# Attention in two blocks: two other strings for the order of TensorE's visits and of the projections in the first block

## The chip, the cores and the metric

The kernel runs on one core of one Trainium2 chip. The metric is the device time of one execution in microseconds (us); lower is better. TensorE multiplies matrices into PSUM (8 banks), ScalarE and VectorE read PSUM, GpSimd works on SBUF, and SyncE issues the DMAs in one queue.

## What is computed

Two independent attention layers with 2048 tokens, width 512 and 32 heads of 16 dimensions; the outputs stand side by side. Layer A sees a sliding window of 256 tokens, layer B sees all tokens.

```python
qkv = (x @ wqkv).reshape(B, S, 3, H, Dh)          # S 2048, H 32, Dh 16
scores = einsum("bhqd,bhkd->bhqk", q, k) * Dh**-0.5
mask = (i - j >= 0) & (i - j < 256)               # layer A alone
p = softmax(scores)
out = einsum("bhqk,bhkd->bhqd", p, v) ... @ wo
```

## The kernel before, in words

**Two stages.** In the first block TensorE does layer A's attention and the projections (q, k, v) of both layers. Then a loop does layer B's attention with an order of its own (the strings `MANY`, `FEW`, `OUTS`, `ENDS`). The change touches the first block alone.

**A string sets TensorE's order.** `ORDER_A` has 761 letters, and each letter is one visit of TensorE. The loop over it takes the letters one by one and emits that visit's matmuls; nothing is reordered afterwards.

- `p`: one projection, 12 matmuls of 128x512 on the whole array (line 309). It takes the next name of `ORDER_P`.
- `g`: a quarter of two projections at once, 12 matmuls on the two halves of the array (line 444). Four `g` make two projections; it takes two names.
- `m`: scores for the row maxima, 2 matmuls into two banks (line 607; the first ones of layer B, also `e`, line 561). VectorE then copies under a mask and reduces (lines 616, 617).
- `t`: two small transposes of a unit's maxima (line 681). ScalarE copies the result to `ntr` (line 683), and two DMAs of SyncE (line 688) put it as three extra rows into the q tile `oq`.
- `s`: scores of a pair of heads into two banks (line 717), which need those rows of `oq`. ScalarE takes the exponential (line 724), GpSimd masks it.
- `w`: weights times values, on column groups of the array (line 764).

A unit is one group of four heads and one chunk of 512 queries; layer A has 32 units. Each has one `t`, six `s`, three `w` and eight `m`. Names such as `Av21` in `ORDER_P` read: layer A, v, chunk 2, tile 1; `Ak02` is k of heads' group 0, chunk 2.

**What follows from the order.** The same walk over the string emits the work of the other engines: when a projection ends, ScalarE copies it out of its bank, VectorE or GpSimd splits it, SyncE stores it; loads are emitted when the kernel's own clock (class `Model`) says that they are due. So the two strings also decide where in the queues of ScalarE, VectorE, GpSimd and SyncE each of these stands, and which of the 7 free banks a visit writes. Each queue is worked off in order. `m` and `s` take two banks each, so three such visits fill six of the seven.

Of the kernel before, what the change touches and what calls it, by code (L numbers as in the profile page):

```python
# [57 lines left out]
FILL = 16  # L58
WARM = 22
ORDER_P = (  # L60
# [4 lines left out]
    "Bq20 Bq12 Bk30 Bk31 Bk10 Bq33 Bq30 Bq31 Bk32 Bq32 Bk33 Bk21 ").split()  # L65
WAKE = 200
GAP_V = 1500
PIECE = 4
# [4 lines left out]


ORDER_A = (
    "pppppppppppmmmmpmmgmgmptmgmgmmpmsgmsgmmpmsgmsgmwtsmgmsgmmpmsgsmgmtwwmmmpsmgmsgmswwmsgmsgmmpmssptwsmg"
    "msgmswsmgsmgmmwwmgmsgmstwmsgmsgmmwtsgmsgmswmsgmsgmswmmmpssmtwwmspmsmwssmgsmgmswtmsgsmgmwsmswssmwmmmp"
    "mtmswmsswmsmpsmmpsmwtmmmpsmswmmspmsmwsmsmwwtmsmsmsmpmsmtwsmsmwsmmswssmwmmspmmswsmwtsmgmsgmswsmgsmtgm"
    "mwsmwsmmswsmsmpsmmwmswtmsmwsmmmpmsssmmwsmsmwtmmmpsmswmsmsmwtsmsmwsmmpmmswsmtwmmmpmsgmsgmswtsmgmswpsm"
    "gsmwwmsgmmgmpmsgmsgsmwwtsmgmsgmswsmgsmgmmwtsgsmgsmwwmsgmsgmgsmgmswsmgmmgmwsmwtmsgmsgmswtmsgsmgmswwsm"  # L80
    "gmsgmswsmgsmgsmtwwmmmpmsmpmsmwsmmswtmsgmsgmswsmgsmgsmwmsmtwsmmswssmwmmmpmssmtwswmmmpmsgsmgsmwwmsgsmg"
    "etwmmmpmsgmsgmswsegsmgegesgmswsmgesgemtwmmpmsmwmswmsgsmgestwmsgesgmmpemmpmsmwwtemmpsmgmsgsmwmgegsewm"
    "mmpesstwmgmsgeswsmgsmgsmwesgsmgsmwmgsmgmswesmpsmmwtwmmmpmmmwp")
LAND = 400
LAND_V = 0
LGAP = 2500
# [1296 lines left out]
```

## Time and profile before

| what | value |
|---|---|
| device time, median of 3 runs | 1776.86 us (1775.77 to 1780.85) |
| device time of the profiled execution | 1775.89 us |
| its span | 1774.2 us |
| TensorE busy | 1756.8 us (99%) |
| VectorE busy | 1527.2 us (86%) |
| ScalarE busy | 1402.2 us (79%) |
| GpSimd busy | 648.5 us (37%) |
| TensorE's granted clock | full in each of the 40 slices |

A matmul counts as busy from its start to its modelled end, and neighbours overlap, so a share of 99% does not say that TensorE never waits. The length of a visit is better read as the time from its first matmul's start to the next visit's first start. A row of the timeline has its start, its length, the engine, the line, the operation and what was merged (xcount); in brackets stands idle time ahead of it and what ended that.

### The profile page before, as it was taken

How to read it: one execution, taken by the hardware profiler on the slowest of the kernel's cores; microseconds unless marked ns; L12 is line 12 of the kernel's file. 1: busy time of each engine (PE TensorE's matmuls, PEld its weight loads, DVE VectorE, ACT ScalarE, POOL GpSimd, SP SyncE). 2: the span in 40 equal slices, each digit the busy share in tenths (PEclk: the TensorE clock that was granted, in tenths of full speed). 3: DMA queues.
4: the chain of work that ended last, by engine and by line, in shares of the span. 5: the costliest groups of instructions: out<-in, count | busy, mean ns of one | idle time of the engine just before them, and what ended most of it. 6: DMA issues, size and time to landing. Idle time of an engine off the chain costs nothing.

```text
span 1774.2 us, 38875 instructions
## 1 busy us (share of the span) xinstructions
PE 1756.8 (99%) x14774; PEld 912.2 (51%) x14774; DVE 1527.2 (86%) x2386; ACT 1402.2 (79%) x2749; POOL 648.5 (37%) x1334
## 2 busy tenths in 40 slices
PE   8999999999999999999999999999999999999999
PEld 6776657767754444444444444444444444444456
DVE  4766786676779999999999999999999999999921
ACT  4466676665569888888889999999999999899894
POOL 0377888655755441222201123231112322121420
PEclk9999999999999999999999999999999999999999
DMA  8865667645663224111310311120031131010012
GB/s 267 200 210 199 206 206 223 177 146 163 201 181 108 66 86 89 41 41 41 83 37 17 77 29 30 47 62 17 17 78 35 30 65 38 17 38 26 20 44 102
DMA packets 129354, 166.78 MB, mean 94 GB/s; under 512 B 23204, under 2 KB 59044, under 8 KB 129156
## 3 DMA queue, kind: packets, MB, share of 16 engines
q1 hardware_dynamic: 129168, 164.31, 31.8%
q8 instruction: 116, 1.90, 0.5%
q14 instruction: 70, 0.57, 0.1%
HBM read 94.49 MB, written 68.19 MB: 92 GB/s over the span
## 4 chain that ended last, share of the span: by engine, by line
PE 89%; DVE 4%; DMA 2%; ACT 1%; SPq 1%; issue 1%; POOL 1%; POOLq 0%; ACTq 0%; DVEq 0%
PE ps_all L749 28%; PE ps_all L717 19%; PE ps_all L561 18%; PE ps_all L444 11%; PE ps_all L309 6%; PE ps_all L764 4%; DVE mt L564 3%; PE ps_all L607 3%; ACT p L724 1%; DMA in<-xT_A 1%; DVE nm L617 1%; PE ps_all L681 0%; SPq L473 0%; DVE ps_all L616 0%; DMA parts<-st 0%
## 5 line engine op out<-in xcount | busy, mean ns | idle before, releaser
L724 ACT ACTIVATE p<-ps_all 128x512 f32<-128x512 f32 x2432 | 1262.9, 598 | 204.8 <-PE ps_all L717 137.6
L564 DVE TENSOR_REDUCE mt<-ps_all 128x1 f32<-128x512 f32 (+1 forms) x1658 | 1212.7, 808 | 33.1 <-PE ps_all L561 28.0
L717 PE MATMUL ps_all<-oq,opk 51*128 51x512 f32 (+2 forms) x2752 | 756.9, 401 | 4.0 <-ACT p L724 2.0
L561 PE MATMUL ps_all<-opk,oq 48*128 48x512 f32 x2016 | 661.2, 435 | 0.2
L749 PE MATMUL ps_all<-p,vt 128*17 128x512 f32 (+1 forms) x5488 | 571.0, 490 | 0.0
L717 PEld LDWEIGHTS ps_all<-oq,opk 51*128 51x128 f32 x2752 | 385.8, 185 | 219.2 <-ACT p L724 142.7
L561 PEld LDWEIGHTS ps_all<-opk,oq 48*128 48x128 f32 x2016 | 304.6, 184 | 273.4 <-DVE mt L564 164.7
L735 POOL TENSOR_SCALAR_AFFINE_SELECT p<-p 128x256 f32<-128x256 f32 x480 | 179.0, 408 | 110.0 <-ACT p L724 107.4
L749 PEld LDWEIGHTS ps_all<-p,vt 128*17 128x17 f32 x5488 | 93.6, 95 | 214.2 <-issue 201.4
L616 DVE COPY_PREDICATED ps_all<-mone,ps_all 128x256 f32<-128x256 uint16 x224 | 95.3, 425 | 82.6 <-PE ps_all L607 75.9
L617 DVE TENSOR_REDUCE nm<-ps_all 128x2 f32<-128x512 f32 x224 | 155.2, 693 | 7.7
L633 POOL TENSOR_TENSOR mu<-mt 128x16 f32<-128x16 f32 x31 | 6.9, 222 | 409.9 <-DVE mt L564 409.9
L635 POOL TENSOR_TENSOR mu<-mt,mm 128x16 f32<-128x16 f32 x62 | 13.6, 220 | 388.7 <-DVE mt L564 388.7
L444 PE MATMUL ps_all<-x,w 64*128 64x512 f32 x720 | 119.2, 392 | 0.0
L444 PE MATMUL ps_all<-w_o,x_o 64*128 64x512 f32 x576 | 110.2, 394 | 0.0
L309 PE MATMUL ps_all<-x,w 128*128 128x512 f32 x408 | 102.7, 400 | 2.4 <-ACT x L257 1.7
L764 PE MATMUL ps_all<-p,vt 128*17 128x384 f32 (+2 forms) x1408 | 94.1, 386 | 0.1
L607 PE MATMUL ps_all<-opk,oq 48*128 48x384 f32 (+2 forms) x512 | 92.1, 361 | 2.0 <-DMA oq<-parts 0.5
L803 POOL TENSOR_TENSOR rd<-ld,minus 128x32 f32<-128x32 f32 x15 | 81.9, 5459 | 19.6 <-DMA ld<-od 19.6
L444 PEld LDWEIGHTS ps_all<-x,w 64*128 64x128 f32 x720 | 84.4, 185 | 8.9
L309 PEld LDWEIGHTS ps_all<-x,w 128*128 128x128 f32 x408 | 74.2, 188 | 24.8 <-ACT p L724 2.9
L392 ACT ACTIVATE raw<-ps_all 128x512 f32<-128x512 f32 x56 | 32.2, 596 | 68.5 <-PE ps_all L309 53.6
(79 smaller groups left out, 1042.7 us busy)
## 6 DMA issues: line engine op xcount, KB each, us to landing
parts<-st SPq DMA_DIRECT2D x64, 512.0 KB
oq<-parts SPq DMA_DIRECT2D x128, 128.0 KB
opk<-parts SPq DMA_DIRECT2D x128, 128.0 KB
od<-ou SPq DMA_DIRECT2D x64, 256.0 KB
vd<-vst SPq DMA_DIRECT2D x32, 272.0 KB
oq<-parts SPq DMA_DIRECT2D x128, 64.0 KB
opk<-parts SPq DMA_DIRECT2D x128, 64.0 KB
t<-od SPq DMA_DIRECT2D x32, 256.0 KB
```

Source lines behind the costliest of these rows:

```text
L309: nc.tensor.matmul(ps, l(u), r(v), start=start and k == 0, stop=stop and k == n - 1)
L444: op = nc.tensor.matmul(ps[a ^ turn], l(u)[rows], r(v)[rows], start=turn == q == 0, stop=turn == 1 and q == 11)
L561: nc.tensor.matmul(ps[:, a - lo], q[rows, 128 * qt:128 * qt + 128], k[rows, kc * QC:kc * QC + QC], start=True, stop=True)
L564: op = nc.vector.tensor_reduce(out=m[:, kc, lo:lo + len(sides), r, qt], in_=ps, axis=AX.X, op=ALU.max)
L607: nc.tensor.matmul(two[:, a, 0:w], opq[b, g, c][rows, r, 128 * qt:128 * qt + 128], opk2(g)[rows, r, t0:t1], start=True, stop=True)
L616: nc.vector.copy_predicated(two[:, :, 256:384], later, two[:, :, 0:128])
L617: op = nc.vector.tensor_reduce(out=m[:, :, r, qt, 0], in_=two[:, :, 128:384], axis=AX.X, op=ALU.max)
L717: nc.tensor.matmul(ps[x][:, col:col + n1], opk2(g)[rows, pr, 128 * k:128 * k + 128], opq[b, g, c][rows, pr, q0:q0 + n1], start=True, stop= ...
L724: op = nc.scalar.activation(p[:, a0 + x, :w], ps[x][:, :w], AF.Exp, scale=SCALE)
L735: nc.gpsimd.affine_select(out=v, in_=v, pattern=[[0, 2], [sign, 128]], compare_op=ALU.is_ge, fill=zero_fill, base=base, channel_multiplier ...
L749: nc.tensor.matmul(o[32 * j:32 * j + VW, q0:q1], vt[(g // 2) % 2][:, kt, vc:vc + VW], pts[1, g, c, kt, j // 2][:, j % 2, q0:q1], start=kt ...
L764: nc.tensor.matmul(o[32 * j:32 * j + VW, q0:q0 + w], vt[(g // 2) % 2][:, kt, vc:vc + VW], pts[b, g, c, m, j // 2][:, j % 2, col:col + w], ...
```

## The change

`ORDER_P` and `ORDER_A` are two other strings. Both orders have the same letters (280 `m`, 192 `s`, 96 `g`, 96 `w`, 48 `p`, 33 `t`, 16 `e`) and the same 96 names of projections; nothing else in the file differs. The two first lines of each show the kind of edit:

```diff
 ORDER_P = (
-    "Aq00 Ak00 Ak01 Av11 Av02 Av03 Aq01 Av01 Ak02 Av21 Av13 Aq02 Av12 Av00 Aq03 Ak03 Av20 Av10 Av33 Ak20 Av32 "
+    "Aq00 Ak00 Aq01 Av13 Av01 Av03 Aq02 Ak01 Av11 Av20 Av12 Ak02 Av02 Av00 Aq03 Ak03 Av23 Av31 Av21 Aq12 Av30 "
...
 ORDER_A = (
-    "pppppppppppmmmmpmmgmgmptmgmgmmpmsgmsgmmpmsgmsgmwtsmgmsgmmpmsgsmgmtwwmmmpsmgmsgmswwmsgmsgmmpmssptwsmg"
+    "ppppppppmmpmmppmgmmgmptmgmmgmppsmgsmgmmpmsgmsgmtwmsgmsgmmpmsgmsgmtwwmmmpmsgmsgsmwwmsgmsgmmpssmptwmsg"
```

After the first block the rows of every engine are the same in both programs, up to the numbers of buffers.

**TensorE near the start, before.** The last of eleven projections in a row (L309), then the first `m` (L607), for the first unit's q tile.

```order
L309 MATMUL ps_all<-w_v_225,x_2_3_255 128x512 x3
L309 MATMUL ps_all<-w_v_207,x_1_0_168 128x512 x3
L309 MATMUL ps_all<-w_v_210,x_1_1_171 128x512 x3
L309 MATMUL ps_all<-w_v_222,x_1_2_189 128x512 x3
L309 MATMUL ps_all<-w_v_225,x_1_3_192 128x512 x3
L607 MATMUL ps_all<-opk_75,oq_0_0_268 128x128 x4
L607 MATMUL ps_all<-opk_75,oq_0_0_268 128x256 x4
L309 MATMUL ps_all<-x_2_0_239,w_0_0_139 128x512 x3
L309 MATMUL ps_all<-x_2_1_242,w_0_0_139 128x512 x3
L309 MATMUL ps_all<-x_2_2_252,w_0_0_139 128x512 x3
L309 MATMUL ps_all<-x_2_3_255,w_0_0_139 128x512 x3
L607 MATMUL ps_all<-opk_75,oq_0_0_268 128x384 x4
```

**The same place after.** Four `m` now stand in pairs between projections, the first pair behind the eighth projection.

```order
L607 MATMUL ps_all<-opk_75,oq_0_0_268 128x128 x4
L309 MATMUL ps_all<-w_v_207,x_1_0_168 128x512 x3
L309 MATMUL ps_all<-w_v_210,x_1_1_171 128x512 x3
L309 MATMUL ps_all<-w_v_222,x_1_2_189 128x512 x3
L309 MATMUL ps_all<-w_v_225,x_1_3_192 128x512 x3
L607 MATMUL ps_all<-opk_75,oq_0_0_268 128x256 x4
L309 MATMUL ps_all<-w_v_207,x_2_0_239 128x512 x3
L309 MATMUL ps_all<-w_v_210,x_2_1_242 128x512 x3
L309 MATMUL ps_all<-w_v_222,x_2_2_252 128x512 x3
L309 MATMUL ps_all<-w_v_225,x_2_3_255 128x512 x3
L309 MATMUL ps_all<-w_v_207,x_1_0_168 128x512 x3
```

The two first pairs moved apart, and earlier: one projection now stands between them, where before they followed each other.

**TensorE at the unit whose q tile is `oq_2_2` (heads' group 2, chunk 2), before.** The `t` of this unit (L681), then seven `s` and `m` in a row, then a projection.

```order
L681 MATMUL ps_all<-ident,nm_74 32x128
L607 MATMUL ps_all<-opk_75,oq_2_3_2210 128x384 x2
L717 MATMUL ps_all<-oq_2_1_1854,opk_75 128x256 x4
L607 MATMUL ps_all<-opk_75,oq_2_3_2210 128x384 x2
L717 MATMUL ps_all<-oq_2_1_1854,opk_75 128x256 x4
L607 MATMUL ps_all<-opk_75,oq_2_3_2210 128x384 x2
L717 MATMUL ps_all<-oq_2_1_1854,opk_75 128x384 x2
L717 MATMUL ps_all<-oq_2_1_1854,opk_75 128x128 x2
L607 MATMUL ps_all<-opk_75,oq_2_3_2210 128x384 x2
L309 MATMUL ps_all<-x_2_0_239,w_3_0_1298 128x512 x3
```

**The same `t` after.** Values (L764) now stand between the `s` and `m` that follow it.

```order
L681 MATMUL ps_all<-ident,nm_74 32x128
L717 MATMUL ps_all<-oq_2_1_1858,opk_75 128x128 x2
L717 MATMUL ps_all<-oq_2_1_1858,opk_75 128x384 x2
L607 MATMUL ps_all<-opk_75,oq_2_3_2205 128x384 x4
L717 MATMUL ps_all<-oq_2_1_1858,opk_75 128x128 x2
L717 MATMUL ps_all<-oq_2_1_1858,opk_75 128x384 x2
L764 MATMUL ps_all<-p_2_0_1_0_2371,vt_78 17x384 x2
L764 MATMUL ps_all<-p_2_0_1_1_2378,vt_78 17x384 x2
L607 MATMUL ps_all<-opk_75,oq_2_3_2205 128x384 x2
L717 MATMUL ps_all<-oq_2_1_1858,opk_75 128x256 x4
```

The run of seven is broken. The first `s` with this unit's rows follows 25 rows further on before, and 36 after.

**TensorE a little later, after.** The `t` of the next unit (`oq_2_3`) and one visit of values are followed by eight `s` and `m` in a row.

```order
L717 MATMUL ps_all<-oq_2_2_2036,opk_75 128x128 x2
L717 MATMUL ps_all<-oq_2_2_2036,opk_75 128x384 x2
L607 MATMUL ps_all<-opk_76,oq_3_0_2451 128x256 x2
L717 MATMUL ps_all<-oq_2_2_2036,opk_75 128x128 x2
L717 MATMUL ps_all<-oq_2_2_2036,opk_75 128x384 x2
L607 MATMUL ps_all<-opk_76,oq_3_0_2451 128x256 x2
L717 MATMUL ps_all<-oq_2_2_2036,opk_75 128x256 x4
L607 MATMUL ps_all<-opk_76,oq_3_0_2451 128x384 x2
L717 MATMUL ps_all<-oq_2_2_2036,opk_75 128x256 x4
L607 MATMUL ps_all<-opk_76,oq_3_0_2451 128x384 x2
L764 MATMUL ps_all<-p_2_1_2_0_2552,vt_78 17x384 x2
```

Before, that `t` and its `w` were followed by four `s` and `m` up to the next `w`; now it is eight.

## Rows read from the trace of the kernel before

**Rows 1.** Busy time of each engine before and after the first block's last matmul; clock, DMA

```profile
core 0: us, PE busy (x) PEld busy (x) DVE busy (x) ACT busy (x) POOL busy (x), PEclk, DMA share, GB/s
0.00:515.60 515.60, 504.61 (x4520) 359.46 (x4520) 357.35 (x763) 303.15 (x605) 330.08 (x644) 1.00 0.65 198
515.60:1774.00 1258.40, 1252.23 (x10255) 552.75 (x10254) 1169.85 (x1623) 1099.09 (x2144) 318.47 (x690) 1.00 0.19 51
```

**Rows 2.** TensorE's timeline: the block's first matmul and the loop's first one

```profile
6.70 0.50 PE L309 MATMUL ps_all<-x,w 128*128 128x512 f32 x1 [1.15 <-ACT x L257]
...
515.62 0.50 PE L717 MATMUL ps_all<-oq,opk 51*128 51x512 f32 x2
```

**Rows 3.** TensorE's timeline, a stretch without crowding; start, length, what

```profile
218.63 0.50 PE L717 MATMUL ps_all<-oq,opk 51*128 51x256 f32 x4
218.97 0.40 PE L607 MATMUL ps_all<-opk,oq 48*128 48x384 f32 x2
219.20 1.54 PE L444 MATMUL ps_all<-x,w 64*128 64x512 f32 x12
220.58 0.34 PE L607 MATMUL ps_all<-opk,oq 48*128 48x384 f32 x2
220.75 0.40 PE L717 MATMUL ps_all<-oq,opk 51*128 51x384 f32 x4
220.99 1.60 PE L444 MATMUL ps_all<-x,w 64*128 64x512 f32 x12
...
222.59 0.41 PE L717 MATMUL ps_all<-oq,opk 51*128 51x384 f32 x4
222.93 1.06 PE L764 MATMUL ps_all<-p,vt 128*17 128x128 f32 x16
223.92 0.44 PE L717 MATMUL ps_all<-oq,opk 51*128 51x384 f32 x2
```

**Rows 4.** TensorE's timeline near the start, 30 to 42 us

```profile
30.44 2.88 PE L309 MATMUL ps_all<-x,w 128*128 128x512 f32 x12
33.16 2.88 PE L309 MATMUL ps_all<-w_v,x 128*128 128x512 f32 x12
37.25 3.01 PE L309 MATMUL ps_all<-w_v,x 128*128 128x512 f32 x12 [1.21 <-DVE st L399]
40.19 0.60 PE L607 MATMUL ps_all<-opk,oq 48*128 48x128 f32 x5
...
41.78 3.02 PE L309 MATMUL ps_all<-x,w 128*128 128x512 f32 x12
```

**Rows 5.** Timelines of SyncE, ScalarE and VectorE in the same place

```profile
24.49 2.23 SPq L473 DMA_DIRECT2D opk<-parts  x4
...
33.38 2.41 ACT L257 ACTIVATE x<-in 128x512 fp32r<-128x512 f32 x4 [1.17 <-DMA in<-xT_A]
...
36.51 0.68 DVE L399 TENSOR_TENSOR st<-ps_all,st 128x512 fp32r<-128x512 f32 x1
```

**Rows 6.** Timelines of TensorE and SyncE, and TensorE's waits over the first block

```profile
194.14 0.23 PE L681 MATMUL ps_all<-ident,nm 128*32 128x128 bf16 x2
...
201.40 1.08 PE L764 MATMUL ps_all<-p,vt 128*17 128x128 f32 x16
203.62 0.74 PE L717 MATMUL ps_all<-oq,opk 51*128 51x128 f32 x4 [1.15 <-DMA oq<-ntr]
...
200.74 1.50 SPq L688 DMA_DIRECT2D oq<-ntr  x2
...
PE ps_all L717 <- DMA oq<-ntr: 1.1, 1, 1.1
```

**Rows 7.** TensorE's timeline in a crowded stretch

```profile
194.29 0.45 PE L607 MATMUL ps_all<-opk,oq 48*128 48x384 f32 x2
...
196.97 0.50 PE L717 MATMUL ps_all<-oq,opk 51*128 51x384 f32 x4 [0.48 <-ACT p L724]
...
197.62 3.02 PE L309 MATMUL ps_all<-x,w 128*128 128x512 f32 x12
```

More of the change, by code (lines that the diff above doesn't have):

```diff
@@ L60 @@
 ORDER_P = (
[4 rows of a table removed]
-    "Bq20 Bq12 Bk30 Bk31 Bk10 Bq33 Bq30 Bq31 Bk32 Bq32 Bk33 Bk21 ").split()
[4 rows of a table added]
+    "Bq22 Bq10 Bq23 Bk30 Bq30 Bq31 Bk31 Bk32 Bk10 Bq33 Bq32 Bk33").split()
 WAKE = 200
@@ L75 @@
 ORDER_A = (
-    "pppppppppppmmmmpmmgmgmptmgmgmmpmsgmsgmmpmsgmsgmwtsmgmsgmmpmsgsmgmtwwmmmpsmgmsgmswwmsgmsgmmpmssptwsmg"
[L77 to L83, printed above, removed]
+    "ppppppppmmpmmppmgmmgmptmgmmgmppsmgsmgmmpmsgmsgmtwmsgmsgmmpmsgmsgmtwwmmmpmsgmsgsmwwmsgmsgmmpssmptwmsg"
+    "msgmswsmgsmgmmwwmsgsmgmstwmsgmmgwsmgmsgmswtsmgmsgsmwsmmpmswtwsmmpsmsmwmsgmsgmswtmsgsmgmwsmswsmsmwmsm"
+    "pmmswtmswsmmpmsmpsmtwmmmpmsswmmspmmswtsmmswmsmswsmmpmmswtwsmsmsmsmwmsswmsmpmsmwmswtmsgmgmswsmgmsgmst"
+    "wsmmwsmmswsmmspsmmtwsmwsmmswmmmpmssmsmwsmwsmtmmmpmsswmmstwmsmssmmwmspmmswtmswmmmpmsgmsgmswtmsgmspwms"
+    "wwsmgmgmsgmmpmsgmsgsmwtwmsgmmgswmsgmsgmswsmgmsgsmwtwsmgmsgmgsmgmswsmgmmgmtwmswmsgmsgmstwmsgmsgsmwwms"
+    "gsmgmswsmgsmgmmpmsmwsmtwmsmpmsmwsmwtmsgmsgmswsmgsmgsmwmsmtwsmmswmsswmmmpssmmtwswmmmpmsgsmgsmtwwmsgse"
+    "geswemmpmgsmgmswsegsmgmgmsgeswsegsmgmmtwmmpmsmwmstwesgmsgmswsmgmsgmmpemmpmsmwtwemmpsmgmsgsmwmgmgsmwe"
+    "mmpmsstwegmsgeswsmgsegsewesgmsgsewmgmsgmswmmspmmswtwmmmpmmmpw")
 LAND = 400
```

6 rows, old and new, of the table ORDER_P are left out of this document.

## The prediction

> **What bounds the kernel now.** I read the busy times by stage first. Until 515.6 us TensorE is busy for 504.6 us while VectorE has 357.4, ScalarE 303.2 and GpSimd 330.1; the clock is at its upper level (2.4 GHz) throughout [rows 1]. TensorE bounds the first block, and the others only through waits that they put into its order. The loop behind it has the same rows in both programs, so its 1258.4 us should stay, whatever the block gives [rows 1]. The block itself lasts from 6.70 to 515.62, 508.9 us [rows 2]; that is all that the change can touch.
>
> Next I took prices from TensorE's timeline, as the time from one visit's start to the next one's. In a calm stretch `g` costs 1.38 (219.20 to 220.58), `m` 0.17 (220.58 to 220.75), `s` 0.24 (220.75 to 220.99) [rows 3]. Changing the kind of matmul costs extra: an `s` just behind a `t` takes 0.34 (218.63 to 218.97), an `s` just ahead of a `w` 0.34 (222.59 to 222.93), both 0.10 more, and `w` between such visits 0.99 [rows 3]. A `p` followed by a `p` costs 2.72 (30.44 to 33.16), followed by an `m` 2.94 (37.25 to 40.19) [rows 4]. So a run of `p` adds 0.10 + 0.22 + 0.10 = 0.42 us to what it does, and a run of `w` and `t` 0.20 (the price of `w` holds the rest).
>
> With these prices the block without a single wait is 96 x 1.38 + 48 x 2.72 + 296 x 0.17 (`m`, `e`) + 192 x 0.24 + 80 x 0.99 + 16 x 0.50 (the `w` with half the matmuls, taken at half) + 38 x 0.42 + 86 x 0.20 = 480 us (small `s` and `m` counted in full, `t` at nothing). 38 and 86 are the runs in the string. The trace has 508.9, so about 29 us are waits, and only these and the number of runs can shrink.
>
> **The change, part by part.**
>
> *Changes of kind.* The same letters, so the same visits. Counted in the strings, runs of `w` and `t` are 86 before and 86 after; runs of `p` are 38 and 39. That is one more at 0.42: **+0.4 us**. The order does not win by fewer changes of kind.
>
> Each `p` matmul brings its own weights, and twelve take 2.72, 0.227 each [rows 4]. The Trainium skill (TensorE: Matmul & The Clock Gate, "The mechanism" in Part 3) says that a weight load overlaps with running matmuls only where the row groups differ. By its figure for a load of 128 columns (128/1.2, 107 ns; "LDWEIGHTS" there), an estimate for a `p` would be 12 x (0.227 + 0.107) = 4.0 us, and a change of kind would then cost nothing of its own: this term would be 0 instead of +0.4. The trace disagrees: loads are hidden inside a `p`, and 0.10 shows where the kind changes [rows 3, 4]. I go by the rows.
>
> *The start.* Before, eleven `p` stand in a row. The tenth starts at 33.16 and would end at 35.88, but the eleventh starts at 37.25, when VectorE's subtraction (36.51, 0.68 long) has freed the bank that it writes: 1.37 us lost [rows 4, 5]. That subtraction was late because ScalarE, at 33.38, first waited for a load of x and split four tiles, with the copy of the ninth projection behind them; the eleventh writes the ninth's bank [rows 5]. Then four `m` in a row take 40.19 to 41.78 = 1.59 us, where prices give at most 4 x 0.17 + 0.10 + 0.10 = 0.88: 0.7 lost, since eight banks' worth of maxima meet seven banks [rows 4]. After, the copy of the eighth `p` stands ahead of those splits in ScalarE's queue, two `m` stand behind it, and each pair of `m` is followed by 2.7 to 2.9 us of `p`. I take both waits as gone: **-1.4 and -0.7 us**. The bounds: nothing gone (0) if the next bank is late instead. The first `m` now comes at about 30.4 instead of 40.19, and needs the k rows whose four DMAs are issued from 24.49 to 26.7 [rows 4, 5]; that leaves 3.7 us. No row shows their landing; from the nearest one, rows issued at 200.74 are used at 203.62, 2.9 us later [rows 6]. So I take no wait, and +1.2 (the longest wait for a load in these rows [rows 5]) as the other bound.
>
> *Late rows.* An `s` needs three rows that go from its unit's `t` over ScalarE and SyncE. For the unit of `oq_2_2` the `t` is at 194.14, SyncE issues the rows only at 200.74, behind other DMAs, and the `s` comes at 203.62, 9.48 us after the `t` [rows 6]. The `w` ahead of it lasted 2.22 (201.40 to 203.62) instead of 0.99: 1.2 lost [rows 6]. After, the visits between this `t` and this `s` are worth 9.5 us by the prices above (6.3 before), so **-1.2 us**. In return four other units get less room: 5.2, 5.6, 5.9 and 5.4 us (chunk 1 of group 1, chunks 0 and 3 of group 2, chunk 1 of group 3). A distance like that is enough when SyncE is free: the `s` at 223.92, 5.3 us after its `t` had passed, has no wait ahead of it [rows 3]; and in the whole block an `s` waited for its rows once [rows 6]. I take a third of one such wait, **+0.4**. Bounds: 0, and 15.9 if all four had the lag of 9.48 (4.3 + 3.9 + 3.6 + 4.1).
>
> *Crowded stretches.* The rest of the waits, 29 - 1.4 - 0.7 - 1.2 = 26 us, is mostly where `s` and `m` follow each other without a `p`, `g` or `w`. From 194.29 to 197.62 seven of them take 3.33 us, where prices give 4 x 0.17 + 3 x 0.24 + 0.20 = 1.60: 1.7 lost, ended by ScalarE's exponentials [rows 7]. Three such visits fill six of seven banks; the fourth waits. So I count visits beyond the third in a run of `s` and `m`: 21 before (12 runs of four, one each of five, six and seven) and 21 after (nine of four, one each of six, seven, eight). The run of seven is broken, but one of eight appears a little later. **0 us**; bounds a quarter of the 26 either way, 6 us, since such waits also depend on what the engines have behind them.
>
> *The sum* is 0.4 - 1.4 - 0.7 - 1.2 + 0.4 = -2.5 us. The profiled execution took 1775.89 us (span 1774.2 and 1.7 around it), which makes 1773.4; the median of the runs lies 1.0 above the profiled one, so I predict **1774.4 us**. A measurement of this kernel tells about 0.3% (5.3 us) from no change, so this counts as no change.
>
> **The rivals.**
>
> *The crowded stretches thin out.* The order spreads `s` and `m` over the queues better than my count shows. For it: these waits are by far the largest item, and a wait there depends on the backlog, which a count of runs does not see. Against it: the numbers of `s` and `m` in each stretch between the `g` are almost those of before. With a quarter of the 26 us gone, 1774.4 - 6 = 1768 us. It decides from about 3 us gained there.
>
> *Slower: rows come late at the four shortened units.* The place is SyncE's queue between `t` and the `s`. For it: at one of the four (`oq_2_3`) the rows are issued behind a store, an output copy and four loads of q. Against it: one such wait in 32 units before [rows 6]. With half of the bound, 8 us, 1774.4 + 8 = 1782 us; it is slower by more than 0.3% once the four together wait for over 8 us.
>
> *Nothing comes of it.* The bank waits at the start come back one visit later, and the end of the block meets a loop whose VectorE is busy for 1169.9 of 1258.4 us [rows 1] and takes back what is left: 1776.9 us.
>
> **How the numbers follow.** The forecast has 0.46, thinner crowded stretches 0.31, nothing 0.13, late rows 0.10. The low end, 1767, is the thinning with its quarter and 1 us more; the high end, 1781, takes the k rows late at the start (+1.2) and 5 us of late rows. Beyond it lies most of the late rows' case, and below it the tail of the thinning. Faster by over 0.3% (under 1771.5) takes the first rival and a little of the forecast: 0.33; slower (over 1782.2) 0.09; within 0.3% 0.58.
>
> **What would show it.** In the profile after, the loop's first L717 should start 2 to 3 us before 515.6, with the loop as long as before. The mark "DVE st L399" of 1.21 us near 37 us should be gone, the first L607 stand near 30.4 without a wait for DMA. One wait of L717 for "oq<-ntr" at most, and not at 203. Stretches where `s` and `m` crowd should have waits for "p L724" and "nm L617" of about the same sum. The prediction is wrong if the block is shorter by more than 5 us, which the crowded stretches alone can give, or if "oq<-ntr" shows several waits.

## The result: no gain, 4 us longer, and the profile after

The changed kernel takes 1782.13 us (median of 10 executions, 1778.68 to 1783.83), before 1778.3 us (10 executions measured beside it): ratio 1.0023, interval 1.0014 to 1.0033. The forecast was 1774.4, and 1782.1 lies above its range. The profiled execution took 1781.72 us, with a span of 1780.0. That of before took 1775.89, which is 2.4 us under the median of its ten, so the two traces lie further apart (5.8 us) than the medians (3.8 us).

Busy time, clock and DMA ahead of and behind the block's last matmul, after, as in [rows 1]:

```profile
0.00:520.70 520.70, 508.93 (x4520) 361.93 (x4520) 357.53 (x763) 302.44 (x605) 331.19 (x644) 0.99 0.65 197
520.70:1780.00 1259.30, 1252.08 (x10260) 553.12 (x10254) 1169.94 (x1623) 1099.58 (x2144) 319.54 (x690) 1.00 0.19 51
```

The loop is as long as before (1259.3 against 1258.4), so the loss is in the block, and the mean clock in the block is 0.99. The first block's timeline of TensorE after, as in [rows 2, 4, 6]:

```profile
5.84 0.79 PE L309 MATMUL ps_all<-x,w 128*128 128x512 f32 x1
...
30.45 0.44 PE L607 MATMUL ps_all<-opk,oq 48*128 48x128 f32 x4
30.82 2.99 PE L309 MATMUL ps_all<-w_v,x 128*128 128x512 f32 x12
33.74 0.51 PE L607 MATMUL ps_all<-opk,oq 48*128 48x256 f32 x4
34.17 3.02 PE L309 MATMUL ps_all<-w_v,x 128*128 128x512 f32 x12
37.48 3.02 PE L309 MATMUL ps_all<-w_v,x 128*128 128x512 f32 x12 [0.29 <-DVE st L399]
...
47.49 0.23 PE L681 MATMUL ps_all<-ident,nm 128*32 128x128 bf16 x2
...
52.23 5.75 PE L309 MATMUL ps_all<-x,w 128*128 128x512 f32 x24
60.98 0.65 PE L717 MATMUL ps_all<-oq,opk 51*128 51x384 f32 x3 [3.00 <-DMA oq<-ntr]
61.70 3.03 PE L444 MATMUL ps_all<-w_v,x 64*128 64x512 f32 x12
64.45 0.93 PE L717 MATMUL ps_all<-oq,opk 51*128 51x384 f32 x3
...
520.75 0.50 PE L717 MATMUL ps_all<-oq,opk 51*128 51x512 f32 x2
```

The block lasts 520.75 - 5.84 = 514.9 us instead of 508.9 [rows 2]; of these 6.0 us, 0.9 is its earlier first matmul alone (5.84 against 6.70), since the eighth projection ends at the same time in both traces (the next visit starts at 30.45 after, at 30.44 before [rows 4]). What was forecast for the start is there: the first `m` at 30.45 waits for no DMA, the four `m` take 0.37 and 0.43 us in two pairs where they took 1.59, and the bank wait is 0.29 where it was 1.21 [rows 4]. At 47.49 the first unit's `t` stands, 41.65 us into the block (51.37 - 6.70 = 44.67 before); 12 `p` stand ahead of it in the string, where it was 13, and the thirteenth now stands between the `t` and its `s`. Then TensorE stands for 3.00 us ahead of the block's very first `s`, and the `g` behind it takes 2.75 us (61.70 to 64.45) where its price is 1.38 [rows 3].

TensorE's marked waits in the block after, as the last row of [rows 6]; total, times, longest:

```profile
PE ps_all L717 <- DMA oq<-ntr: 3.0, 1, 3.0
PE ps_all L717 <- ACT p L724: 2.0, 4, 0.8
PE ps_all L607 <- ACT p L724: 1.5, 4, 0.5
...
PE ps_all L607 <- DVE nm L617: 0.8, 3, 0.4
```

There is still one wait for rows, but it is no longer the one at 203.62: that is gone, and none stands at the four shortened units.

Where the rows were held shows in SyncE's timeline after, ahead of that `s`:

```profile
45.74 0.71 SPq L367 DMA_DIRECT2D one_d<-vt  x1
49.91 1.21 SPq L463 DMA_DIRECT2D opk<-one_d  x4
...
52.52 1.87 SPq L688 DMA_DIRECT2D oq<-ntr  x2
...
57.46 1.95 SPq L411 DMA_DIRECT2D parts<-st  x2
```

and in SyncE's own waits from 44 to 64 us:

```profile
SPq L463 <- DMA one_d<-vt: 3.4, 1, 3.4
SPq L411 <- DMA opk<-one_d: 2.2, 2, 1.4
```

L367 stores a row of constant ones in DRAM, L463 loads it four times into the k tiles; both are let go once twelve projections have begun. SyncE stands for 3.4 us until that store has landed, and the issues behind it wait for the loads once more. The `t` of the first unit is 3 us earlier in the block than before, ScalarE's copy of it is done at 48.40, but its rows go out only at 52.52. Then they need long, by the chain of waits after:

```profile
52.52 8.42 DMA oq<-ntr
```

Before, SyncE's timeline and TensorE's at the same unit read:

```profile
43.42 0.70 SPq L367 DMA_DIRECT2D one_d<-vt  x1
47.54 1.22 SPq L463 DMA_DIRECT2D opk<-one_d  x4
...
52.26 1.68 SPq L688 DMA_DIRECT2D oq<-ntr  x2
```

```profile
51.37 0.23 PE L681 MATMUL ps_all<-ident,nm 128*32 128x128 bf16 x2
...
58.52 0.61 PE L717 MATMUL ps_all<-oq,opk 51*128 51x384 f32 x3
```

There too the ones went out first, and SyncE stood 3.3 us for their store. The rows went out at almost the same time (52.26, after 52.52), and their `s` is due at almost the same time (58.52; after 57.98, where the projections end). What differs is when the loads of the ones went out: at 47.54 before and at 49.91 after, since their store stands at 45.74 where it stood at 43.42. The rows land behind these loads. By the semaphore events of the two traces, which mark when a DMA has landed, the four loads land one by one (50.96 to 55.92 before, 53.63 to 58.57 after). The first rows land 10.9 us behind the first load's issue in before (58.43) and 11.0 us behind it in after (60.94), though SyncE issued them 4.7 and 2.6 us behind it. So the rows were in time by 0.1 us before; of the 3.0 us that TensorE stands after, 2.4 come from the later loads and 0.5 from the earlier `s`. The hold of 4.1 us that SyncE puts on the rows themselves (48.40 to 52.52) does not set their landing by itself.

The Trainium skill (DMA: Bandwidth & Descriptors, "Anatomy of one DMA") says that DMA engines do not wait on semaphores: the wait is taken on the issuing engine ahead of dispatch. SyncE's 3.4 us agree. By its formula there, 2.0 us + bytes / 436e3, which it gives for DMAs that GpSimd issues, a load of 12 KB would need about 2.0 us, an estimate; the 8.42 us here are four times that, with the DMA engines 0.90 busy from 58.0 to 61.5 us.

A second thing is late by the same queue. ScalarE's timeline after:

```profile
63.31 0.60 ACT L388 ACTIVATE st<-ps_all 128x512 fp32r<-128x512 f32 x1 [7.42 <-DMA parts<-st]
63.81 1.08 ACT L724 ACTIVATE p<-ps_all 128x512 f32<-128x512 f32 x2
```

`st` has two buffers. The third projection of q or k in this stretch finds the first one's store not landed (SyncE issued it at 57.46), and the first exponentials stand behind that copy.

Granted clock in stretches after (busy us of TensorE first, clock third from the end):

```profile
58.00:61.50 3.50, 0.52 (x5) 0.49 (x7) 0.00 (x0) 0.00 (x0) 0.00 (x0) 1.00 0.90 315
61.50:64.90 3.40, 3.40 (x18) 2.79 (x15) 1.81 (x3) 1.58 (x4) 0.00 (x0) 0.50 0.75 226
...
211.70:215.10 3.40, 3.40 (x38) 2.22 (x34) 2.06 (x4) 2.50 (x6) 3.40 (x5) 0.50 0.48 123
```

Three times in the block (the third at 269.7) TensorE had the lower level, 1.2 GHz, for 3.4 us: once behind the 3 us in which it stood, twice behind crowded runs with waits. The trace of before has no such stretch in the block [rows 1], but other executions of before have some: the mean clock is 0.9984 over 132 of them, and 1.000 in the profiled one. That gave two theories: late rows of the first unit (with SyncE's queue as the cause), and the clock.

### The profile page after: what moved, and what is told of

Read it like the earlier page. It is cut to its first block, busy times and chain, and to the rows that moved or that the text cites. A ratio compares the mean times of both kernels' runs of the same rounds, so it can differ in the third digit from the quotient of the medians.

```text
span 1780.0 us, 38875 instructions
## 1 busy us (share of the span) xinstructions
PE 1761.0 (99%) x14774; PEld 915.0 (51%) x14774; DVE 1527.5 (86%) x2386; ACT 1402.0 (79%) x2749; POOL 650.7 (37%) x1334
## 4 chain that ended last, share of the span: by engine, by line
PE 90%; DVE 4%; DMA 2%; ACT 1%; POOL 1%; issue 1%; SPq 1%; POOLq 0%; ACTq 0%
PE ps_all L749 28%; PE ps_all L561 18%; PE ps_all L717 18%; PE ps_all L444 11%; PE ps_all L309 6%; PE ps_all L764 5%; PE ps_all L607 3%; DVE mt L564 3%; DMA in<-xT_A 1%; ACT p L724 1%; DMA parts<-st 1%; PE ps_all L681 1%; DMA oq<-ntr 0%; DVE nm L617 0%; SPq L473 0%
## 5 line engine op out<-in xcount | busy, mean ns | idle before, releaser
L617 DVE TENSOR_REDUCE nm<-ps_all 128x2 f32<-128x512 f32 x224 | 155.2, 693 | 7.7
L444 PE MATMUL ps_all<-x,w 64*128 64x512 f32 x792 | 125.3, 391 | 0.0
L764 PE MATMUL ps_all<-p,vt 128*17 128x384 f32 (+2 forms) x1408 | 96.3, 392 | 0.2
L607 PE MATMUL ps_all<-opk,oq 48*128 48x384 f32 (+2 forms) x512 | 92.4, 367 | 3.7 <-ACT p L724 1.5
L309 PE MATMUL ps_all<-x,w 128*128 128x512 f32 x372 | 93.9, 401 | 1.1 <-ACT x L257 0.9
L444 PEld LDWEIGHTS ps_all<-x,w 64*128 64x128 f32 x792 | 89.3, 185 | 9.3
L444 PEld LDWEIGHTS ps_all<-w_o,x_o 64*128 64x128 f32 x576 | 76.2, 186 | 7.2 <-ACT ob L872 0.8
```

Source lines behind the costliest of these rows:

```text
L309: nc.tensor.matmul(ps, l(u), r(v), start=start and k == 0, stop=stop and k == n - 1)
L444: op = nc.tensor.matmul(ps[a ^ turn], l(u)[rows], r(v)[rows], start=turn == q == 0, stop=turn == 1 and q == 11)
L607: nc.tensor.matmul(two[:, a, 0:w], opq[b, g, c][rows, r, 128 * qt:128 * qt + 128], opk2(g)[rows, r, t0:t1], start=True, stop=True)
L617: op = nc.vector.tensor_reduce(out=m[:, :, r, qt, 0], in_=two[:, :, 128:384], axis=AX.X, op=ALU.max)
L764: nc.tensor.matmul(o[32 * j:32 * j + VW, q0:q0 + w], vt[(g // 2) % 2][:, kt, vc:vc + VW], pts[b, g, c, m, j // 2][:, j % 2, col:col + w], ...
```

## The experiments

Every ratio is to before, measured beside it, with its interval. A kernel's file is before or after with the edit shown.

**1. The ones earlier, and the halves of the string.**

```diff
-    list_("load", lambda: nb >= 12, at0, ones_out)
+    list_("load", lambda: nb >= 6, at0, ones_store)
+    list_("load", lambda: nb >= 9, at0, ones_load)
```

The store and the four loads are now two steps, let go at the sixth and the ninth projection; in after (e1) and in before (e2). Two more kernels join the first 64 visits of one string to the rest of the other, with the names of the projections in the order that this gives (e3, e4).

> The changed kernel; the store of the ones and the four loads of them into the k tiles are let go after 6 and 9 projections instead of both after 12, nothing else. Theory 1: the first unit's rows land late (60.9 us) because their DMAs stand in SyncE's queue behind the wait for that store, and then on the same DMA engines behind these four loads. Then TensorE's 3.0 us wait for oq<-ntr and the half-clock stretch behind it go: the loop starts 4 to 5 us earlier, 1777.5 to 1778.5 us, ratio to before 0.9995 to 1.0003. Rival, theory 2: the crowded stretches at 205 to 275 us and their half-clock stretches cost what was lost: 1781 to 1782.5, ratio 1.0015 to 1.0023.

> The kernel before with the same move of the store and the loads of the ones. There the rows landed at 58.4 us, when TensorE came to them, so both theories expect no change: 1778 us, ratio 0.999 to 1.0005. If the loads cost something in their new place (they now share the queue with the loads of x), it shows here as 1 to 2 us more.

> The first 64 visits and 22 projections in the order before, the rest in the changed order (three projections that would come twice are taken in the rest's place for the missing ones). Theory 1 (the loss is in the first 64 visits): 1777.5 to 1779.5 us, ratio 0.9995 to 1.0008. Theory 2 (the loss is in the crowded stretches later): 1781 to 1783, ratio 1.0015 to 1.0025.

> The other half: the first 64 visits and 22 projections in the changed order, the rest in the order before. Theory 1: as slow as the change or slower, 1781.5 to 1783.5 us, ratio 1.0018 to 1.003, with the wait for oq<-ntr of about 3 us and a stretch at half clock near 61 us. Theory 2: 1777 to 1779, ratio 0.9995 to 1.0005.

Measured: e1 1.0024 (1.0012 to 1.0036), e2 1.0008 (0.9999 to 1.0017), e3 1.0019 (1.0007 to 1.0031), e4 1.0015 (1.0006 to 1.0023). In e1 the wait for rows is gone, but another took its place, in TensorE's waits (this file has two lines more, so L609 is the `m`):

```profile
PE ps_all L609 <- ACT vst L510: 3.6, 1, 3.6
```

The ones now stood ahead of stores of v, whose buffers ScalarE waits for. So e1 moves the hold in the queue and does not remove it. Neither half of the string alone is as quick as before. For e3 I found no clean reason. It has the start of before, its first `s` has no wait for rows, and 1.0019 is what theory 2 gave for it; its trace has 10.2 us of the lower clock (from 209.7 and 271.1 us) where after has its crowded stretches, but it is the trace of one of its slower executions (1783.21 us; median 1780.41). The seam moves three projections as well.

**2. Waits filled with repeated products, and the ones at the very start.** In e5 and e6 the visits ahead of a wait do their products several times, with the same result:

```diff
+AGAIN = {167: 3, 195: 4, 207: 2, 239: 3, 245: 5, ... 335: 15, 346: 3, 355: 2, 360: 4, 362: 3}
-        for a in range(2):
+        for a in [0, 1] * times():
-            for x in range(heads):
+            for x in list(range(heads)) * (1 if b else times()):
```

In e7 the ones go out behind the loads of x's second piece and of wv; e8 has both edits.

> The kernel after, in which 18 visits that stand just ahead of a wait of 0.3 us or more in its crowded stretches (visits 167 to 362 of the string) do their products two to fifteen times over, with the same result each time, so that TensorE works through the wait instead of standing; the repeats are sized to end within the wait, and nothing else moves. Clock theory: after is longer because TensorE's clock falls to 1.2 GHz for 3.4 us at a time just behind those stretches (near 211 and 270 us in its trace and in two of its variants); with the waits filled these two half-clock stretches go, the mean granted clock rises by about 0.002, and the time falls by 2 to 3.4 us: ratio to before near 1.0007, from 1.0023. Wait theory: after is longer by its waits alone, and the clock follows the chip and not the order; then the clock stays near 0.997 and the ratio at 1.0023, or a little above where a repeat outlasts its wait.

> The kernel before with the same edit at its own 16 visits ahead of a wait of 0.25 us or more (visits 170 to 363). Clock theory: the executions of before differ among themselves by 0 to 5 half-clock stretches (mean granted clock 1.000 to 0.995, and about 1.4 us for each 0.001); filled waits take away those behind the crowded stretches, so the mean clock rises from 0.998 towards 0.999 or 1.000 and the median falls by 0.7 to 2 us: ratio 0.9990 to 0.9996. Wait theory: ratio 1.0000 to 1.0003, clock unchanged.

> The kernel after, with the store of the constant ones issued behind the loads of x's second piece and their four loads behind those of wv, within the first 13 us, where it was the twelfth projection that let them go (they stood in SyncE's queue ahead of the first unit's rows and were still on their way as these were). Theory of the first unit's rows: the wait of 3.0 us for these rows ahead of the first score, and the half-clock stretch that follows it, both go, since in the run with the ones moved to the sixth and ninth projection they only pushed other stores of SyncE back: time down by 2 to 4 us, ratio 1.0000 to 1.0012. Rival: the start is set by the loads and by SyncE's queue as a whole, so that another wait takes the place of this one: ratio stays at 1.0018 to 1.0028.

> Both edits on the kernel after: the ones within the first 13 us, and the 18 visits ahead of waits repeated. If the clock theory and that of the first unit's rows both hold, the gains add: no half-clock stretch but those in which the loads hold TensorE up at the start, mean clock 0.999 to 1.000, ratio 0.9985 to 0.9997, which is faster than before by the 0.7 to 1.4 us that the start was forecast to give. If only one holds, ratio 1.0003 to 1.0012; if neither, 1.0023.

Measured: e5 1.0047 (1.0033 to 1.0060), e6 1.0007 (0.9997 to 1.0016), e7 1.0044 (1.0027 to 1.0061), e8 1.0053 (1.0039 to 1.0067). All missed. At half of the 18 places of e5 the repeat did not end within the wait. TensorE's timeline around visit 335 in e5, and the same place in after:

```profile
255.02 0.30 PE L607 MATMUL ps_all<-opk,oq 48*128 48x128 f32 x1
255.58 1.89 PE L607 MATMUL ps_all<-opk,oq 48*128 48x128 f32 x29 [0.26 <-ACT p L724]
257.20 0.61 PE L717 MATMUL ps_all<-oq,opk 51*128 51x128 f32 x4
```

```profile
252.81 0.30 PE L607 MATMUL ps_all<-opk,oq 48*128 48x128 f32 x1
253.37 0.32 PE L607 MATMUL ps_all<-opk,oq 48*128 48x128 f32 x1 [0.26 <-ACT p L724]
253.85 0.55 PE L717 MATMUL ps_all<-oq,opk 51*128 51x128 f32 x4 [0.16 <-ACT p L724]
```

From the first of these `m` to the `s` it is 2.18 us; in after, without repeats, 1.04 (252.81 to 253.85). In both the visit's second matmul waits for its bank, 0.56 us behind the first. The 28 repeats come behind that wait, where only 0.48 us were left to fill, so most of the time in which TensorE stood here could not be had for nothing. In e6 the mean clock of the executions rose to 0.9995 (0.9984 in before's), and the time did not fall. In e7 the ones stood ahead of loads of x and stores of v:

```profile
PE ps_all L309 <- ACT vst L508: 5.0, 1, 5.0
```

**3. The loads of the ones behind the rows.**

```diff
-    list_("load", lambda: nb >= 12, at0, ones_out)
+    list_("load", lambda: nb >= 12, at0, ones_store)
+    list_("ones", lambda: (max_rows, 0, 0, 0) in made, at0, ones_load)
```

The store stays where it was; the four loads go out once the first unit's `t` is made, behind its rows. In after (e9) and in e4's mixed string (e10). In e11 the repeats stand at nine places alone, and e12 is e9 with these.

> The kernel after, in which the four loads of the ones go out behind the first unit's rows in SyncE's queue, and no longer ahead of them; the store of the ones stays at the twelfth projection, so no earlier store is pushed back (in the trace of after SyncE stood from 46.5 to 49.9 us for that store and then issued the loads, while the rows were ready at 48.4 and went out at 52.5). Theory of the first unit's rows: they go out some 3 to 4 us earlier and land before 58 us, so that the wait of 3.0 us ahead of the first score goes, and with it the half-clock stretch behind it: time down by 2.5 to 4 us, ratio 1.0000 to 1.0009. Rival (the start is set by the loads as a whole, and the score then waits for the ones instead): ratio 1.0016 to 1.0028.

> The first 64 visits of after and the rest of before (measured at 1.0015), with the loads of the ones behind the first unit's rows. Theory of the first unit's rows: the start then keeps what it gained (2.6 us ahead of before at the twentieth visit) and the rest has before's clock: 2.5 to 4 us off, ratio 0.9992 to 1.0001. Rival: 1.0010 to 1.0020.

> The kernel after with repeats at nine visits only (167, 239, 245, 260, 261, 263, 312, 360, 362): those at which the trace of the run with eighteen showed that the repeat ended within the wait; at the others the wait began only when the repeated product was done, so that the repeat was paid in full, some 4 us in all. Clock theory: half-clock stretches behind the crowded stretches are fewer, mean clock up by 0.001 to 0.002 over after's 0.9966, and time down by 1.5 to 3.4 us, ratio 1.0004 to 1.0015. Wait theory (the clock costs nothing that the waits would not): ratio 1.0020 to 1.0026.

> Both of the last edits on after: the loads of the ones behind the first unit's rows, and the nine free repeats. If both theories hold, the gains add to 4 to 7 us: ratio 0.9985 to 1.0000, mean clock 0.999 or above. If only the rows' theory holds, 1.0000 to 1.0009; if only the clock's, 1.0004 to 1.0015.

Measured: e9 1.0004 (0.9995 to 1.0013), e10 0.9999 (0.9989 to 1.0008), e11 1.0025 (1.0015 to 1.0035), e12 1.0004 (0.9995 to 1.0014). This is the edit that gives the loss back: after falls from 1.0023 to 1.0004, 3.4 us, and the mixed string from 1.0015 to 0.9999. SyncE in e9:

```profile
47.92 1.73 SPq L688 DMA_DIRECT2D oq<-ntr  x2
49.75 1.33 SPq L463 DMA_DIRECT2D opk<-one_d  x4
...
53.08 2.46 SPq L411 DMA_DIRECT2D parts<-st  x2
```

TensorE in e9, the `t`, the two projections and the first `s`:

```profile
46.67 0.23 PE L681 MATMUL ps_all<-ident,nm 128*32 128x128 bf16 x2
...
50.76 5.75 PE L309 MATMUL ps_all<-x,w 128*128 128x512 f32 x24
56.44 0.50 PE L717 MATMUL ps_all<-oq,opk 51*128 51x384 f32 x4
```

and ScalarE in e9:

```profile
58.71 0.60 ACT L388 ACTIVATE st<-ps_all 128x512 fp32r<-128x512 f32 x1 [4.28 <-DMA parts<-st]
```

The rows go out 1.25 us behind the `t` (5.03 after) and, by the semaphore events, land 2.5 us later (50.45), where they took 8.42 us behind the loads of the ones. The `s` follows the projection without a mark, and the stores of `parts` go out 4.4 us earlier than in after. What is left of the second wait is 4.28 of 7.42 us. What was expected of the clock did not come: the trace of e9 has the lower level as long as that of after, 10.2 us in the block, and again behind the first scores.

```profile
61.60:65.00 3.40, 3.40 (x14) 2.75 (x12) 2.14 (x5) 0.31 (x1) 1.13 (x3) 0.50 1.00 289
...
208.40:215.20 6.80, 6.80 (x52) 3.56 (x54) 2.65 (x5) 4.66 (x9) 6.24 (x14) 0.50 0.69 215
```

The loop still starts 2.7 us earlier in it (518.04 against 520.75), so in this pair of traces the gain is not the clock's. The filled waits do not shorten the kernel, with or without this edit (e11 beside after, e12 beside e9).

**4. Is the third projection's buffer the rest? And the control in before.** Names `Av00` and `Aq03` change places, so that projections of q and k end at visits 21, 27 and 30 and no longer at 27, 29 and 30: with the ones behind the rows in after (e13) and in the mixed string (e14), alone in after (e16). e15 is before with the ones behind the rows.

```diff
-    "... Av12 Ak02 Av02 Av00 Aq03 Ak03 Av23 ..."
+    "... Av12 Ak02 Av02 Aq03 Av00 Ak03 Av23 ..."
```

> The kernel after with the loads of the ones behind the first unit's rows (measured at 1.0004) and with the names Av00 and Aq03 exchanged, so that projections of q and k end at visits 21, 27 and 30 and not at 27, 29 and 30. Theory of the two st buffers: ScalarE's copy then finds a free buffer, its wait of 4.3 us for a store of parts goes, and with it the waits of 1.3 and 0.8 us of the first scores for the exponentials behind it: 1.5 to 2.5 us off, ratio 0.9990 to 0.9997. Rival: the stores of SyncE take the next place (q's fourth piece is needed only at visit 49), or the exchanged projection waits for x's fourth piece: ratio 1.0003 to 1.0012.

> The first 64 visits of after and the rest of before with the loads of the ones behind the rows (measured at 0.9999), and the same two names exchanged. Theory of the two st buffers: 1.0 to 2.5 us off, ratio 0.9985 to 0.9994, faster than both kernels. Rival: 0.9998 to 1.0006.

> The kernel before with the loads of the ones behind the first unit's rows. Its rows land at 58.43 and 58.62 us, when its first score, at 58.52, is due. Theory of the first unit's rows: they come 2 to 4 us earlier and nothing waits for them, so that the time is the same where the rows are in time anyway and up to 1 us less in executions where they are not: ratio 0.9994 to 1.0000. Rival: moving these loads changes the clock or other transfers by itself, whichever string it stands in: ratio 0.9985 or below, or above 1.0005.

> The kernel after with the two names exchanged alone; the loads of the ones stay ahead of the rows. Theory of the first unit's rows: the wait of 3.0 us stays, and the waits for the two st buffers, which here lie partly behind it, go: 0.5 to 1.5 us off, ratio 1.0014 to 1.0021. If instead most of the loss hangs on the st buffers, ratio 1.0000 to 1.0008.

Measured: e13 1.0008 (0.9998 to 1.0018), e14 1.0003 (0.9994 to 1.0012), e15 1.0014 (1.0005 to 1.0023), e16 1.0032 (1.0019 to 1.0045). The exchange gives no gain in any of three kernels. It does not settle what the two buffers cost, because it left most of ScalarE's wait where it was: 2.86 of 4.28 us in the trace of e13, 6.37 of 7.42 in that of e16. The control missed as well: in before, whose rows were not held, the same edit costs 2.5 us (0.9 to 4.1). Why is open. Moving these loads is no gain by itself; it paid only in the two strings whose rows were late. With the loads moved, the two strings are alike within their intervals (e9 and e15).

**5. Late rows in before, and the wait of after filled.** e18 is before with the four loads of the ones issued a second time, to the same places, ahead of the first unit's rows. e17 is after with the first product of visit 30, the projection ahead of that `s`, done eleven times.

```diff
         load_ones(1)
+        [nc.sync.dma_start(opk2(g)[ROW[a] + KS:ROW[a] + KM].bitcast(F32),
+                           one_d.rearrange('(s r) t -> s r t', s=3)) for g in range(2) for a in range(2)]
```

> The kernel after, in which the projection ahead of the first score (visit 30) does its first product eleven times, with the same result; the ten repeats take 2.3 us, which is less than the 3.0 us for which TensorE waits for the first unit's rows behind it. The wait for the rows stays, TensorE works through most of it. Theory that the half-clock stretch behind this wait (61.5 to 64.9 us in the trace of after) costs about 1.4 us of the 4: the stretch goes, the mean clock rises by about 0.001 and the time falls by 1.0 to 1.7 us, ratio 1.0013 to 1.0018. Rival (the wait alone costs, the clock falls elsewhere as often): ratio 1.0021 to 1.0026.

> The kernel before, with the four loads of the ones issued a second time behind the first, to the same places with the same content; the string is that of before. In SyncE's queue the first unit's rows then stand behind eight loads and not four. Theory of the first unit's rows: they land 1 to 4 us later than the 58.4 and 58.6 us of before, the first score waits for them as long, and the time rises by that and by up to 1.4 us of half clock: ratio 1.0006 to 1.0030. Rival (this wait is hidden by what ScalarE and the loads owe anyway): ratio 0.9995 to 1.0004.

Measured: e18 1.0024 (1.0014 to 1.0034), e17 1.0021 (1.0012 to 1.0030). e18 loses in before, with its own string, as much as the change did. SyncE and TensorE in e18, whose trace is that of its slowest execution (1787.74 us; median 1780.82):

```profile
51.46 3.91 SPq L370 DMA_DIRECT2D opk<-one_d  x4
...
56.77 2.07 SPq L688 DMA_DIRECT2D oq<-ntr  x2
```

```profile
52.13 0.23 PE L681 MATMUL ps_all<-ident,nm 128*32 128x128 bf16 x2
...
62.85 0.85 PE L717 MATMUL ps_all<-oq,opk 51*128 51x384 f32 x2 [3.42 <-issue]
```

The rows go out 4.6 us behind the `t` (0.9 in before, 5.0 in after), and the first `s` comes 3.42 us late. The mark names no releaser; by the semaphore events the two DMAs of rows land at 62.76 and 62.95 us (58.43 and 58.62 before), so the rows fit as the last to come. The loads of weights stand behind the added loads too, and e18 shows the price of a held queue at this place, not that of the rows alone.

TensorE in e17, the filled projection, the first `s`, the `g` behind it and the next `s`:

```profile
52.51 8.00 PE L309 MATMUL ps_all<-x,w 128*128 128x512 f32 x34
60.51 0.67 PE L717 MATMUL ps_all<-oq,opk 51*128 51x384 f32 x3
...
61.15 1.69 PE L444 MATMUL ps_all<-w_v,x 64*128 64x512 f32 x12
63.90 0.94 PE L717 MATMUL ps_all<-oq,opk 51*128 51x384 f32 x3 [1.06 <-ACT p L724]
```

The standing is filled, the granted clock stays 1.00 from 61.5 to 64.9 us, and the twelve matmuls of the `g` take 1.69 us where they took 3.03 after; but the next `s` now waits 1.06 us for ScalarE, whose copy into `st` starts at 62.77 (63.31 after), when the first store of `parts` has landed (62.66 by the semaphore events; the copy's mark names VectorE's L617, which ended then too). From the first `s` to this next one it is 3.39 us, and 3.47 in after: the half-clock stretch between them cost next to nothing, because ScalarE was the one to wait for. The ratio is that of after within the intervals.

## Why the prediction was wrong, point by point

- **The start, -1.4 and -0.7.** Right in mechanism: the bank wait fell by 0.92 (1.21 to 0.29), two thirds of the 1.4, and the four `m` by about 0.8 (1.59 to 0.37 + 0.43). The k rows were in time, as taken; two later `m` waited 0.2 us each for theirs.
- **Late rows, -1.2 and +0.4.** The wait at `oq_2_2` went, and the four shortened units wait for nothing. But **this is the step that failed**: it looked at units whose distance from `t` to `s` in TensorE's prices grows or shrinks, and held that such a distance is enough when SyncE is free. The first unit's distance grew (7.15 us before, 51.37 to 58.52; 10.5 after up to the end of the projections, 47.49 to 57.98), so it was not looked at. What its rows wait for is not in that distance: they land behind the loads of the ones, which hang on a count of projections and on a store that SyncE waits for, and these went out 2.4 us later than before. The one margin that mattered was 0.1 us before (rows landed at 58.43, `s` at 58.52). Those rows were late by 3.00 us, where the sum has +0.4 for all rows that come late anew, and the stores of `parts` were held with them. Experiment 3 shows that with this hold taken away the changed string loses nothing that can be told from before (1.0023 with it, 1.0004 without), and experiment 5 that such a hold makes before as long as after (1.0024). That the hold is the whole of the loss is not shown: e3 has no late rows and is at 1.0019, and the edit that helps after makes before longer (e15).
- **The gain at the start did not come through.** In after the 3.00 us stand behind it. In e10, the start of after without the hold and the rest of before, -2.1 us would be 0.9988, and it is at 0.9999 (0.9989 to 1.0008); as the same edit costs before 2.5 us, it stays open what the start is worth.
- **Crowded stretches, 0 within 6.** The marked waits for exponentials and maxima went from 2.8 us (2.0 + 0.2 and 0.3 + 0.3) to 4.3 (2.0 + 1.5 and 0.8): within the bounds, on the bad side. With the same start and the loads moved, the rest of after and the rest of before are alike within their intervals (e9 1.0004, e10 0.9999).
- **Changes of kind, +0.4.** No run isolates it. As a whole, -2.5 us would be 0.9986; without the hold the changed string is at 1.0004 (0.9995 to 1.0013) beside before. Beside before with the same loads moved (e15, 1.0014) its ratio is lower by 0.0010, 1.8 us, and the two intervals together leave room for nothing and for -2.5.
- **The base.** The sum starts from the median of three executions, 1776.86; that of the ten measured beside after is 1778.3. So 1.4 of the 7.7 us between 1774.4 and 1782.1 are the base, and the other 6.3 are a gain of 2.5 that did not come and a loss of 3.8.
- **The rivals.** The slower one named the right kind of wait at the wrong units, none of which waited; that its 1782 us is the measured time is luck. "Nothing comes of it" is near what the string is worth with the loads moved, but not for its reasons: the bank wait did not come back at its full length (0.29 us), and the loop took back nothing (1259.3 against 1258.4).

The clock theory is neither shown nor excluded. Filling the waits raised the mean clock in e6 and e11 (0.9984 to 0.9995, 0.9966 to 0.9978) and left the time where it was or longer, but the repeats take time of their own, so this does not price the clock. Taken by equal mean clock, after is 1.9 us longer than the 132 executions of before (1782.9 against 1781.0 at 0.996, 1781.3 against 1779.3 at 0.997), half of the 3.8 us between the medians; the other half goes with after's lower mean clock (0.9966 against 0.9984). Whether late rows and crowded stretches bring the clock down, or the chip does, no run settles; e9's is higher again (0.9982).

It stays open how the 3.4 us of experiment 3 split into the wait, the clock, and ScalarE's wait for `parts`; e17 says that filling the wait and keeping the clock up behind it gives back at most some 2 us, with ScalarE's copy only 0.5 us earlier. Open is also why e3 is slow, and why the ones behind the rows cost before its 2.5 us. No version that I ran is faster than before beyond its interval.

## What to carry to other kernels

When an order on one engine is changed, look at each in-order queue that its results pass, and at what stands there by a trigger of its own (a count, a clock): a result lands behind the transfers ahead of it, and where these go out later, it is late even if it was made earlier. Look first at the places that were only just in time before (by 0.1 us here), not at those whose distance shrinks. A store followed by a load of the same bytes holds an issuing queue for the store's whole landing, 3.4 us here, so put what others need next ahead of that load. Measure such a move in each string: the one that gave after 3.4 us back cost before 2.5.

## What the runs showed of the hardware that I had not expected

- Executions of one kernel differ by the clock's half stretches. The 132 executions of before that the experiments were measured beside, by mean granted clock of the span:

```
clock   executions   mean us
1.000       35       1775.6
0.999       31       1776.5
0.998       33       1778.2
0.997       26       1779.3
0.996        5       1781.0
0.995        2       1783.3
```

  About 1.4 us for each 0.001, and one stretch of 3.4 us at 1.2 GHz is 0.001 of this span (3.4 / 2 / 1776). After's ten executions had 0.996 to 0.998, e9's eleven 0.997 to 1.000.
- Repeated products fill only what lies behind them: at visit 335 the `s` came 1.14 us later for 28 repeated matmuls, though TensorE had stood there for 0.9 us (1.04 less two matmuls of 0.06), since half of that lay ahead of the repeats.
- Two loads of rows of 12 KB took 8.42 us from issue to use behind four loads of 48 KB and two of 256 KB, and landed in 2.5 and 2.1 us where they went out ahead of the four (e9).
